# Last stores off GpSimd, two sums of one block on VectorE, one pair of loads on SyncE: attention and two MoE layers

## The chip, the cores and the metric

The kernel runs on one core of a Trainium2 chip. The time is that of one execution on the device in microseconds (us). TensorE (PE) multiplies matrices; VectorE (DVE), ScalarE (ACT) and GpSimd (POOL) compute on tiles; SyncE (SP), ACT and POOL issue the DMAs here.

## What is computed

Attention without a square score matrix, then two pairs of dense layers, on 4608 tokens (8 batches of 576), all in float32:

```
q_s = softmax(q over head_dim);  k_s = softmax(k over seq)
kv  = einsum('bhsd,bhse->bhde', k_s, v)
x   = einsum('bhsd,bhde->bhse', q_s, kv)  -> tokens x 512
h   = x @ moe_w_in   (512 -> 2048);  g = relu(h) ** 2;  y = g @ moe_w_out
h2  = y @ moe2_w_in  (512 -> 2048);  g2 = silu(h2);     out = g2 @ moe2_w_out
```

## The kernel before

Every float32 matrix is split into a high and a low part of a shorter type, and a product is three matmuls: high by high, low by high, high by low. The casts that make the high parts stand on ACT (names `ah`, `wh`, `wT`), the differences that make the low parts on DVE (`al`, `wl`, again `wT`).

**Stage one** is attention and the first dense layer, in NB = 9 blocks of tokens (i = 0 to 8), each NF = 16 steps on PE (`h<-x,wh` and its like). Beside the steps of a block run the attention of the next one and the work on the hidden layer of this one. A step's result goes through relu and square on ACT into a tile `gs` with seven slots: four quarters A11, A12, A21, A22 and three sums. The next layer multiplies in a scheme with seven products of quarters, and it wants these operand sums made beforehand: `g_first` (DVE) makes S1 = A21 + A22 and S3 = A11 − A21, `g_second` makes S2 = S1 − A11 and S4 = A12 − S2 on GpSimd, and `g_store` sends the tile, 896 KB, to DRAM (`g1d0` to `g1d7`) by a DMA that GpSimd issues. There are eight such pairs of sums a block, j = 0 to 7, at due steps 2j + 3, 2j + 4 and 2j + 5. Three tiles with two halves each are used in turn, so the ACT result of a later j waits until the store of an earlier one has landed. The last block's sums run on past the last step, into the next stage.

**The later stages** are the first layer's output (`x<-al,wT`, `d<-ah,wB`, steps of PE on stored tiles that come back by SP as `al<-g1d`), the second layer's input and its output. Here `wT`, `wB` and `wN` are weight sums; the raw ones (`wt`, `wB`) are made by GpSimd and DVE, and a low part is made by ACT and DVE just before its use. 

**The end.** The result of the last tokens comes back in two halves; each half is transposed by DVE into `st` and written by `store()` in 16 DMAs, over segments, quarters a and rows r. When `ends` is true (the last tokens), before gave four of them to GpSimd, and six each to ACT and SP; half 1 goes some 8 us ahead of half 0. Eight semaphores stand for the DMAs of SP and ACT together, so from the fifth store on a queue each waits for the landing of an earlier one.

**The start.** `r_load` brings the last 64 keys and values of every head of a batch (`kr`, `vr`); for batch 0 the two `kr` loads are issued by GpSimd and the two `vr` loads by ACT, ahead of the list `first_loads` ("q0 k1 v0 q1 w0 ...") on SP and ACT.

**The order.** Block 0 of stage one is ordered by a scheduler, which may move instructions on the engines for the sake of their inputs. From block 1 on, `pinned` keeps every instruction in the order in which the program issues it. All instructions are recorded by the helper `InOrder`, so they all carry its line, L73; closing ones carry L1276 (L1277 with the change), and tile names tell them apart.

Of the kernel before, what the change touches and what calls it, by code (L numbers as in the profile page):

```python
# [13 lines left out]
ALU = mybir.AluOpType  # L14
# [11 lines left out]
def kernel(  # L26
# [36 lines left out]
    class InOrder:  # L63
# [16 lines left out]
    ve, ac, gp, sp, pe = (  # L80
        InOrder(e) for e in (nc.vector, nc.scalar, nc.gpsimd, nc.sync, nc.tensor)
    )
# [7 lines left out]
    NB = NT // TB  # L90
# [31 lines left out]
    def room(dt=F32, name="u"):  # L122
        n = rooms.popleft()
        t = (upool if n < NU else rpool[0]).tile([P, TB], dt, tag=f"u{n}", name=name)
        lent[id(t)] = (t, n, rooms)
        return t
# [29 lines left out]
    S4, S2, S1, A21, A11, A22, A12 = range(7)  # L156
# [231 lines left out]
    def r_load(b, pr, dma=sp, dma2=sp):  # L388


        prs = range(KC)
        held[b] = [room(F32, "kr"), room(F32, "vr")]
        kr, vr = held[b][0], held[b][1][:, 0:KC * (D + 1)]
        n = len(prs)
        kr = kr.rearrange("p (c h d) -> p c h d", c=n, h=2)
        vr = vr.rearrange("p (c d) -> p c d", c=n)
        ms = ve if b == 0 else gp
        for j in range(2):
            ms.memset(kr[SR * j:SR * (j + 1), :, 1 - j, :], LOW)
        ms.memset(vr[:, :, D:D + 1], 1.0)  # L400
        for t, x in ((kr, k), (vr, v)):
            for j in range(2):
                o = slice(SR * j, SR * (j + 1))
                (dma if x is k else dma2).dma_start(
                    out=t[o, :, j, :] if x is k else t[o, :, 0:D],
                    in_=x[b, 2 * prs[0] + j:2 * prs[-1] + 2:2, SM:S, :].rearrange(
                        "c p d -> p c d"
                    ),
                )
        for c, x in enumerate(prs):  # L410
            krt[b, x], vrt[b, x] = kr[:, c], vr[:, c]

    def kv_load(b, pr, dma=sp):
        if pr == 0 and b > 0:
            kvf_room(b)
        hs = slice(2 * pr, 2 * pr + 2)
        kk = room(F32, "k")
        held[b, pr] = [kk]
        if b == 0:
            t = room(F32, "m")  # L420
            held[b, pr].append(t)
            m, mb = t[:, 0:2 * D], t[:, 2 * D:4 * D]
            v_rooms(b, pr)
        else:
            m, mb = input_room(b, pr)[:, 4 * D:6 * D], None
        kk = kk.rearrange("p (h r d) -> p h r d", h=2, r=R)
        dma.dma_start(out=kk, in_=k[b, hs, 0:SM, :].rearrange("h (p r) d -> p h r d", r=R))
        kt[b, pr] = kk
        if b > 0 and pr == 0:
            r_load(b, pr)  # L430
        mt[b, pr], mbt[b, pr] = m, mb
# [294 lines left out]
    def g_place(i, j):  # L726
        n = turns.index(j if i is None else (i, j))
        return g_tiles[n // 2 % 3][:, :, n % 2 * HB:(n % 2 + 1) * HB]
# [16 lines left out]

    def g_second(i, j):
        t = g_place(i, j)
        gp.tensor_tensor(t[:, S2], t[:, S1], t[:, A11], op=ALU.subtract)
        gp.tensor_tensor(t[:, S4], t[:, A12], t[:, S2], op=ALU.subtract)

    def g_store(i, j):
        o = slice(A21, 7) if i == 0 else slice(0, A21 + 1) if i is None else slice(0, 7)
# [25 lines left out]
    for i in range(NB):  # L778
        for j in range(NG):
            if i:  # L780
                at(i, 2 * j + 3, g_first, i, j)
                at(i, 2 * j + 4, g_second, i, j)
            at(i, 2 * j + (5 if i else 3), g_store, i, j)
            if (i, j) in AGAIN:
                again = AGAIN[i, j]
                at(i, 2 * j + 2, g_again, again)
                at(i, 2 * j + 5, g_first, None, again)
                at(i, 2 * j + 6, g_second, None, again)
                at(i, 2 * j + 7, g_store, None, again)
# [39 lines left out]
    def width(u):  # L829
        return sizes[u] * 2 * Q  # L830
# [87 lines left out]
    def hidden_after(ph, u, n, k, j):  # L918
# [39 lines left out]
        elif n == 5:  # L958
# [8 lines left out]
            def then():  # L967
                ve.tensor_tensor(at_("s1"), at_("c21"), at_("c22"), op=ALU.add)
                ve.tensor_tensor(at_("c21"), at_("c11"), at_("c21"), op=ALU.subtract)
                ve.tensor_tensor(at_("s2"), at_("s1"), at_("c11"), op=ALU.subtract)  # L970
                store((A22, "c22"), (S1, "s1"), (S3, "c21"), (A11, "c11"))
# [19 lines left out]
    def out_after(u, n, e, done):  # L991
# [4 lines left out]
        if n == 0:  # L996
            ac.copy(p0, p)
        elif n == 2:
            ac.copy(u2, p)
        elif n == 4:  # L1000
            ve.tensor_tensor(p0, p, p0, op=ALU.add)
            back(ps.pop(("a", e)))
            turn(u, 1, e, p0)
        elif n == 1:
            ac.copy(u3, p)
            d = ps["d", e][:, 0:w]

            def then():
                ve.tensor_tensor(u3, d, u3, op=ALU.add)
                turn(u, 0, 2 + e, u3)  # L1010
            later(then)
        elif n == 6:
            ve.tensor_tensor(u2, p, u2, op=ALU.add)
            back(ps.pop(("d", e)))
            turn(u, 1, 2 + e, u2)
            if e == 1:
                store(u, 1, done)
        elif n == 5:
            turn(u, 0, e, p)
            back(ps.pop(("x", e)))  # L1020
            if e == 1:
                store(u, 0, done)
# [10 lines left out]
    def store(u, half, ends):  # L1033
        w = width(u)
        t = st[half][:, 0:4].rearrange("p n c -> p (n c)")[:, 0:4 * w]
        n = 2 * Q
        for i in range(NB):
            m0, m1 = (max(0, min(w, i * HB + x - starts[u])) // n for x in (0, HB))
            if m0 == m1:
                continue  # L1040
            if i < B:
                lo = i * S + 2 * (starts[u] + m0 * n - i * HB)
                os = [(0, Q, out[lo:lo + 2 * n * (m1 - m0)].rearrange(
                    "(m j s r) (a f) -> a s r j m f", j=Q, s=2, r=2, f=P
                ))]
            else:
                b0 = 2 * ((starts[u] + m0 * n - i * HB) // n)
                rows = out[b0 * S:(b0 + 2 * (m1 - m0)) * S].rearrange(
                    "(m b t) (a f) -> b t m a f", b=2, t=S, f=P
                )  # L1050
                os = [
                    (b * Q // 2, Q // 2, rows[b, SM:S].rearrange("(j s r) m a f -> a s r j m f", s=2, r=2))
                    for b in range(2)
                ]
            for j, nj, o in os:
                for a in range(P // Q):
                    for r in range(2):
                        (gp if not ends or (a, r) in ((0, 0), (2, 1)) else ac if r else sp).dma_start(
                            out=o[a, half, r],
                            in_=t[a * Q + j:a * Q + j + nj].rearrange(  # L1060
                                "j (m r f) -> r j m f", r=2, f=P
                            )[r][:, m0:m1],
                        )
# [23 lines left out]

    warm = [spool.tile([P, 1], F32, name=f"warm{x}") for x in range(3)]
    kv_load(0, 0, ac)
    r_load(0, 0, gp, ac)  # L1090
    ve.memset(warm[0], 0.0)
    ve.memset(warm[2], 0.0)
    gp.partition_all_reduce(warm[1], warm[0], P, bass_isa.ReduceOp.max)
# [58 lines left out]
    for n in range(NB * NF + 6):  # L1152
        i, t = divmod(n, NF)
        ends = i >= NB - 1
# [126 lines left out]
```

## Time and profile before

| | |
|---|---|
| timed runs, median (lowest to highest), us | 1575.15 (1574.21 to 1580.14) |
| the profiled execution's own time, us | 1569.96 |
| its span from the first to the last instruction, us | 1568.1 |
| mean granted clock of PE | 0.994 |
| busy: PE, DVE, ACT, POOL | 97%, 72%, 58%, 40% |
| bytes moved | 419.58 MB, mean 268 GB/s |

The span is what the views of the trace show; the profiled execution's time is 1.86 us longer, and the median of the timed runs 5.19 longer than that. Views are cut to a stretch of time, since the shares of the whole span mix five stages. A row of waits names who waits, for whom, the total, the number and the longest. A row of a timeline gives start, length and, in brackets, the idle time before and what ended it. A group gives its count, busy time, the mean of one in ns, and idle time. PEld is the weight load of PE; a trailing q (SPq) is an engine's sequencer, which issues DMAs and closes the program.

### The profile page before, as it was taken

To read this page: it belongs to the slowest core of one execution; us is meant where nothing else is said; L and a number is where in the kernel's file an instruction comes from. 1 tells how busy PE (TensorE), PEld (TensorE's weight loads), DVE (VectorE), ACT (ScalarE), POOL (GpSimd) and SP (SyncE) were. 2 spreads that over 40 slices of the span, in tenths; PEclk is the share of its full clock that TensorE was granted. 3 is DMA by queue.
4 is the path that set the end of the run, shared out by engine and by line. 5 is a ranking of instruction groups with operands and counts; after the bars stand their busy time and mean duration, and the time that the engine had idled before them with its cause. 6 is when DMAs were issued, how large, how long until landed. Compare 5 with 4: busy or idle time off the path is not lost.

```text
span 1568.1 us, 25313 instructions
## 1 busy us (share of the span) xinstructions
PE 1527.3 (97%) x7679; PEld 1329.8 (85%) x7679; DVE 1125.8 (72%) x2263; ACT 907.0 (58%) x1927; POOL 625.2 (40%) x966
## 2 busy tenths in 40 slices
PE   5899999999999999999999999999999999999996
PEld 3678888888888899999988999999888899889995
DVE  7887888986627977767888776767757865564644
ACT  7876666666545755554575664555646744454431
POOL 1035556655659020211144544445485040605231
PEclk9999999999999999999999999999999999999998
DMA  8969999999977898989996776877889777868761
GB/s 216 287 204 286 310 326 312 328 328 298 333 242 240 292 309 271 331 274 328 304 318 224 245 285 245 297 272 261 310 290 315 235 237 200 247 182 240 207 228 47
DMA packets 270376, 419.58 MB, mean 268 GB/s; under 512 B 70272, under 2 KB 202496, under 8 KB 270240
## 3 DMA queue, kind: packets, MB, share of 16 engines
q1 hardware_dynamic: 216912, 246.39, 51.9%
q0 software_dynamic: 50976, 170.50, 30.0%
q10 hardware_dynamic: 2352, 1.08, 0.3%
q8 instruction: 60, 0.98, 0.3%
q14 instruction: 76, 0.62, 0.1%
HBM read 236.72 MB, written 181.14 MB: 266 GB/s over the span
## 4 chain that ended last, share of the span: by engine, by line
PE 91%; DVE 3%; DMA 2%; ACT 2%; issue 1%; POOL 1%; SPq 0%; POOLq 0%; ACTq 0%; DVEq 0%
PE x L73 37%; PE h L73 23%; PE d L73 19%; PE a L73 9%; PE kvps L73 2%; PE xps L73 2%; DVE wu L73 1%; ACT gs L73 0%; DMA al<-g2d 0%; DMA kr<-in_k_dram 0%; DMA wraw<-in_moe_w_in_dram 0%; DVE al L73 0%; DVE xr L73 0%; DMA g1d<-gs 0%; DMA g2d<-st 0%
## 5 line engine op out<-in xcount | busy, mean ns | idle before, releaser
L73 DVE TENSOR_TENSOR al<-al,ah 128x448 fp32r<-128x448 f32 (+1 forms) x630 | 374.6, 644 | 181.4 <-ACT ah L73 179.2
L73 ACT CAST ah<-al 128x448 fp32r<-128x448 f32 (+1 forms) x630 | 334.6, 577 | 143.6 <-PE x L73 54.1
L73 PE MATMUL h<-x,wh 128*128 128x512 f32 x1152 | 364.3, 396 | 1.3 <-ACT wh L73 0.7
L73 PE MATMUL x<-ah,wT 128*128 128x448 f32 (+1 forms) x960 | 287.3, 370 | 0.0
L73 PEld LDWEIGHTS h<-x,wh 128*128 128x128 f32 x1152 | 214.5, 189 | 47.2 <-ACT wh L73 1.2
L73 ACT COPY st<-x 128x448 f32<-128x448 f32 (+1 forms) x181 | 98.1, 543 | 248.5 <-PE x L73 237.2
L73 PE MATMUL h<-x,wl 128*128 128x512 f32 x576 | 225.9, 392 | 0.0
L73 PEld LDWEIGHTS x<-ah,wT 128*128 128x128 f32 x960 | 180.3, 188 | 19.8 <-ACT st L73 0.7
L73 POOL DMA_DIRECT2D out_dram<-st x184 | 96.6, 535 | 243.5 <-DVE st L73 237.0
L73 POOL DMA_DIRECT2D g2d<-st x262 | 140.8, 542 | 130.4 <-ACT st L73 64.1
L73 PE MATMUL x<-al,wT 128*128 128x448 f32 (+1 forms) x480 | 177.6, 370 | 0.0
L73 POOL TENSOR_TENSOR gs<-gs 128x256 f32<-128x256 f32 x144 | 124.2, 865 | 106.4 <-DVE gs L73 50.9
L73 ACT ACTIVATE gs<-h 128x512 f32<-128x512 f32 x144 | 86.0, 597 | 136.6 <-PE h L73 129.3
L73 PE MATMUL a<-ah,wB 128*128 128x448 f32 (+1 forms) x480 | 148.4, 370 | 0.0
L73 PE MATMUL x<-ah,wB 128*128 128x448 f32 (+1 forms) x480 | 144.7, 373 | 0.0
L73 PE MATMUL d<-ah,wB 128*128 128x448 f32 (+1 forms) x480 | 143.6, 370 | 0.0
L73 PE MATMUL d<-ah,wT 128*128 128x448 f32 (+1 forms) x480 | 143.5, 370 | 0.0
L73 PE MATMUL x<-ah,wN 128*128 128x448 f32 (+1 forms) x480 | 143.5, 370 | 0.0
L73 PEld LDWEIGHTS h<-x,wl 128*128 128x128 f32 x576 | 108.6, 189 | 23.6 <-issue 0.5
L73 DVE TENSOR_TENSOR st<-st 128x448 f32<-128x448 f32 (+1 forms) x161 | 100.0, 647 | 25.9 <-ACT st L73 21.0
L73 DVE TENSOR_TENSOR gs<-gs 128x256 f32<-128x256 f32 x144 | 74.9, 525 | 41.3 <-ACT gs L73 24.0
L73 PEld LDWEIGHTS x<-ah,wB 128*128 128x128 f32 x480 | 90.9, 189 | 9.7
(130 smaller groups left out, 2689.5 us busy)
## 6 DMA issues: line engine op xcount, KB each, us to landing
g1d<-gs POOLq DMA_DIRECT2D x64, 896.0 KB, 6.6
al<-g1d SPq DMA_DIRECT2D x224, 224.0 KB, 4.2
al<-g2d SPq DMA_DIRECT2D x224, 224.0 KB, 3.3
g2d<-st POOLq DMA_DIRECT2D x210, 224.0 KB, 3.7
al<-g1d SPq DMA_DIRECT2D x56, 256.0 KB, 4.2
al<-g2d SPq DMA_DIRECT2D x56, 256.0 KB, 3.1
g2d<-st POOLq DMA_DIRECT2D x52, 256.0 KB, 3.7
al<-x2d SPq DMA_DIRECT2D x56, 224.0 KB, 5.1
```

Of the source, the lines that this page charges most:

```text
L73: got = fn(*a, **kw)
```

## The change

The last tokens' stores go to SP and ACT alone, eight each a half. In the last block (i = 8) both sums of `g_second` stand on DVE. The two loads of the first batch's last keys go first on SP.

```diff
@@ g_second
     def g_second(i, j):
         t = g_place(i, j)
-        gp.tensor_tensor(t[:, S2], t[:, S1], t[:, A11], op=ALU.subtract)
-        gp.tensor_tensor(t[:, S4], t[:, A12], t[:, S2], op=ALU.subtract)
+        by = ve if i == NB - 1 else gp
+        by.tensor_tensor(t[:, S2], t[:, S1], t[:, A11], op=ALU.subtract)
+        by.tensor_tensor(t[:, S4], t[:, A12], t[:, S2], op=ALU.subtract)
@@ store
-                        (gp if not ends or (a, r) in ((0, 0), (2, 1)) else ac if r else sp).dma_start(
+                        (gp if not ends else ac if r else sp).dma_start(
@@ before block 0
     kv_load(0, 0, ac)
-    r_load(0, 0, gp, ac)
+    r_load(0, 0, sp, ac)
```

On POOL, at the end of the last block of stage one (480 to 515 us): `gs x2` are the two sums of one `g_second`, the `g1d` rows are the stores.

```order
 L73 DMA g1d1_128<-gs_186 896x1x256
-L73 TENSOR_TENSOR gs_187<-gs_187 128x256 x2
 L73 DMA g1d2_129<-gs_187 896x1x256
-L73 TENSOR_TENSOR gs_187<-gs_187 128x256 x2
 L73 DMA g1d3_130<-gs_187 896x1x256
-L73 TENSOR_TENSOR gs_188<-gs_188 128x256 x2
 L73 DMA g1d4_131<-gs_188 896x1x256
-L73 TENSOR_TENSOR gs_188<-gs_188 128x256 x2
 L73 DMA g1d5_132<-gs_188 896x1x256
-L73 TENSOR_TENSOR gs_186<-gs_186 128x256 x2
 L73 DMA g1d6_133<-gs_186 896x1x256
```

The sums leave, and the stores follow one another; each now waits for DVE. Ahead of this piece the store of the block before (`g1d7`), that of j = 0 and eight `wt` sums stand in a row, from between which two such pairs have gone.

The sums now stand on DVE, in the same stretch. The piece begins at the `wB` that waits for a `wt` of POOL; before:

```order
L73 TENSOR_TENSOR wB11_5205<-wB11_5205 128x256
L73 TENSOR_TENSOR wB11_5214<-wB11_5214 128x256
L73 TENSOR_TENSOR gs_187<-gs_187 128x256 x2
L73 TENSOR_TENSOR gs_188<-gs_188 128x256 x4
L73 TENSOR_TENSOR al_5352<-al_5352,ah_5440 128x448
L73 TENSOR_TENSOR al_5354<-al_5354,ah_5445 128x448
L73 TENSOR_TENSOR al_5373<-al_5373,ah_5467 128x448
L73 TENSOR_TENSOR al_5375<-al_5375,ah_5472 128x448
L73 TENSOR_TENSOR gs_186<-gs_186 128x256 x2
```

After:

```order
L73 TENSOR_TENSOR wB11_5205<-wB11_5205 128x256
L73 TENSOR_TENSOR wB11_5214<-wB11_5214 128x256
L73 TENSOR_TENSOR gs_187<-gs_187 128x256 x6
L73 TENSOR_TENSOR gs_188<-gs_188 128x256 x6
L73 TENSOR_TENSOR al_5352<-al_5352,ah_5440 128x448
L73 TENSOR_TENSOR al_5354<-al_5354,ah_5445 128x448
L73 TENSOR_TENSOR gs_188<-gs_188 128x256 x2
L73 TENSOR_TENSOR al_5373<-al_5373,ah_5467 128x448
L73 TENSOR_TENSOR al_5375<-al_5375,ah_5472 128x448
L73 TENSOR_TENSOR gs_186<-gs_186 128x256 x2
```

Eight sums become sixteen here. Further on, the last `gs` row ahead of `al_5416` (the `al` that the prediction calls the late one) is `x6` where it was `x2`, the rest stays; from the `wB` to that `al` there are 22 sums where there were 10.

On SP, the end of the program: the last load, then the stores of the two halves (`st_5530`, then `st_5529`).

```order
 L73 DMA al_16111<-g2d3_7_118 128x448
-L73 DMA out_0_dram<-st_5530 32x3x128 x3
-L73 DMA out_0_dram<-st_5530 32x4x128 x3
-L73 DMA out_0_dram<-st_5529 32x3x128 x3
-L73 DMA out_0_dram<-st_5529 32x4x128 x3
-L1276 UNCONDITIONAL_BRANCH
+L73 DMA out_0_dram<-st_5530 32x3x128 x4
+L73 DMA out_0_dram<-st_5530 32x4x128 x4
+L73 DMA out_0_dram<-st_5529 32x3x128 x4
+L73 DMA out_0_dram<-st_5529 32x4x128 x4
+L1277 UNCONDITIONAL_BRANCH
```

Each half has eight stores here in place of six, as on ACT; POOL's end loses its four a half. At the start of SP a row `DMA kr_199<-in_k_dram 64x4x64 x2` stands ahead of all loads, and the scheduler gives block 0 another order: on DVE, `x_335<-xps_332,x_334` of the first pair of heads now stands ahead of the second pair's `sm_345`.

## Rows read from the trace of the kernel before

**Rows 1.** The page's chain that ended last, by engine

```profile
PE 91%; DVE 3%; DMA 2%; ACT 2%; issue 1%; POOL 1%; SPq 0%; POOLq 0%; ACTq 0%; DVEq 0%
```

**Rows 2.** Waits of PE, 90 to 508 us (total, times, longest)

```profile
PE xps L73 <- ACT qh L73: 0.2, 1, 0.2
```

**Rows 3.** Waits of every engine, 490 to 530 us

```profile
ACT ah L73 <- DMA g1d<-gs: 6.8, 1, 6.8
...
PE x L73 <- DVE al L73: 3.5, 1, 3.5
```

**Rows 4.** Two stretches of PE: busy, granted clock, DMA share, GB/s

```profile
511.80:515.10 3.30, 3.30 (x11) 0.50 0.99 308
515.30:518.60 3.30, 3.30 (x18) 1.00 1.01 330
```

**Rows 5.** Timeline of DVE, 482 to 513 us: start, length, idle before

```profile
487.34 3.90 DVE L73 TENSOR_TENSOR wB<-wB 128x256 fp32r<-128x256 f32 x2 [11.22 <-POOL wt L73]
...
509.58 1.78 DVE L73 TENSOR_TENSOR al<-al,ah 128x448 fp32r<-128x448 f32 x1
```

**Rows 6.** Groups on DVE, 486 to 512 us: busy us, mean ns, idle

```profile
L73 DVE TENSOR_TENSOR gs<-gs 128x256 f32<-128x256 f32 x10 | 9.5, 969 | 0.2
L73 DVE TENSOR_TENSOR al<-al,ah 128x448 fp32r<-128x448 f32 x7 | 7.9, 1173 | 0.0
L73 DVE TENSOR_TENSOR wT<-wt,wT 128x256 fp32r<-128x256 f32 x5 | 4.0, 845 | 0.0
```

**Rows 7.** Groups on DVE, 515 to 535 us

```profile
L73 DVE TENSOR_TENSOR al<-al,ah 128x448 fp32r<-128x448 f32 x20 | 12.3, 615 | 0.0
L73 DVE TENSOR_TENSOR wT<-wt,wT 128x256 fp32r<-128x256 f32 x14 | 5.7, 415 | 0.0
```

**Rows 8.** Groups on POOL, 486 to 513 us

```profile
L73 POOL TENSOR_TENSOR gs<-gs 128x256 f32<-128x256 f32 x14 | 12.6, 897 | 0.6
...
L73 POOL TENSOR_TENSOR wt<-wB,wt 128x256 f32<-128x256 f32 x6 | 5.1, 909 | 0.0
```

**Rows 9.** Closing line L1276: ns min/median/max, first and last start

```profile
L1276 SPq EVENT_SEMAPHORE  x11: 17/28/28, 1560.3 to 1568.1; - x11
...
L1276 POOLq DRAIN  x3: 46/102/10698, 1556.7 to 1567.9; - x3
```

**Rows 10.** Waits of PE, 21 to 99 us

```profile
PE xps L73 <- ACT xr L73: 1.8, 1, 1.8
```

**Rows 11.** Timeline of POOL, 1545 to 1570 us

```profile
1546.80 2.19 POOL L73 DMA_DIRECT2D out_dram<-st  x4 [41.01 <-DVE st L73]
```

**Rows 12.** The output's stores, 1540 to 1570 us

```profile
L73 ACTq DMA_DIRECT2D out_dram<-st x12: 323/445/458, 1546.5 to 1557.8; - x12
...
DMA to landing us min/median/max: 1.6/2.9/3.4
```

**Rows 13.** Timeline of ACT, 1545 to 1557 us

```profile
1549.76 1.03 ACT L73 CAST ah<-al 128x448 fp32r<-128x448 f32 x2 [13.59 <-DMA out_dram<-st]
```

**Rows 14.** Timeline of DVE, 1549 to 1552.4 us

```profile
1550.36 1.16 DVE L73 TENSOR_TENSOR al<-al,ah 128x448 fp32r<-128x448 f32 x2 [3.85 <-ACT ah L73]
```

**Rows 15.** Timeline of the weight loads, 1551 to 1552.4 us

```profile
1551.72 0.19 PEld L73 LDWEIGHTS x<-al,wN 128*128 128x128 f32 x1
```

**Rows 16.** Timeline of DVE, 440 to 460 us

```profile
445.64 0.89 DVE L73 TENSOR_TENSOR gs<-gs 128x256 f32<-128x256 f32 x2 [2.88 <-ACT gs L73]
```

**Rows 17.** Timeline of POOL, 480 to 515 us

```profile
482.94 0.82 POOL L73 DMA_DIRECT2D g1d<-gs  x1
...
506.26 0.90 POOL L73 DMA_DIRECT2D g1d<-gs  x1 [0.30 <-DVE wT L73]
```

**Rows 18.** The page's DMA issues: KB each, us to landing

```profile
g1d<-gs POOLq DMA_DIRECT2D x64, 896.0 KB, 6.6
```

**Rows 19.** Tile kr, 0 to 40 us

```profile
L73 POOL DMA_DIRECT2D kr<-in_k_dram x2: 626/694/761, 1.3 to 2.0; - x2
```

**Rows 20.** The chain that ended last, 0 to 36 us: start, length

```profile
2.04 6.95 DMA kr<-in_k_dram
```

## Prediction

> **What bounds the kernel now.** The chain of waits by engine comes first: 91% of the span is PE's own work [rows 1], so a gain on another engine counts only where PE waits for it or where PE is done. The list of PE's waits then tells where those places are. From 90 to 508 us there is nothing above 0.2 us [rows 2]: whatever the start loses or wins goes through to the end one for one. Between 490 and 530 us there is one real hole, where PE waits 3.5 us for an `al` of VectorE, and beside it ScalarE waits 6.8 us for a store of the hidden tiles [rows 3]. The hole has an echo: in the 3.3 us after it the granted clock is 0.50, 1.2 GHz, and 11 matmuls fit in where the next 3.3 us, at 2.4 GHz, hold 18 [rows 4].
>
> Why VectorE is late there is read from its timeline and its groups. It sat 11.22 us behind a `wt` of POOL until 487.34, and the late `al` ends at 509.58 + 1.78 = 511.36; so 24.0 us of work stand between [rows 5]. That work is slow: an `al` takes 1173 ns and a `wT` 845 [rows 6], against 615 and 415 some 20 us later [rows 7], when POOL computes nothing. In the slow stretch POOL ran 14 sums on the hidden tiles, 12.6 us, and its `wt` sums [rows 8]. The two engines slow each other.
>
> The end is the third place. SyncE begins its closing waits, for the stores' landings, at 1560.3, but a DRAIN on POOL that begins at 1556.7 lasts 10,698 ns, to 1567.4 [rows 9]; the span ends 0.7 later, at 1568.1. So the last 6 us hold no work at all. The start is the fourth: PE has single waits of up to 1.8 us before 99 us [rows 10].
>
> The profiled execution took 1569.96 us, its span 1568.1; the median of the timed runs is 1575.15, 5.19 above it. I work in the profiled execution's time and take the difference off the median.
>
> **Part 1, the last stores.** POOL's eight go; its last DMA then ends 41.01 us ahead of 1546.80 [rows 11], and a DRAIN of some 11 us from there is over near 1517, while PE still works. What sets the end instead are the stores of the last half on SyncE and ScalarE, eight each instead of six. ScalarE issues six in the time from 1546.5 to 1549.76 [rows 12, 13], 0.54 each (445 ns for the issue itself, the rest waits for an earlier store). Its last one was issued at 1557.8; two more make it 1558.9, and with the median landing of 2.9 us [rows 12] the data are there at 1561.8. SyncE's closing waits, eleven of 28 ns [rows 9], and the 0.7 of closing make about 1562.8: −5.3. With the longest landing, 3.4, it is −4.8; with an issue every 445 ns, −5.5.
>
> The Trainium skill speaks against this part: "VectorE: DVE Perf Modes", section "The DRAIN you can't avoid", says that the DRAINs of a program's preamble and postamble are about 12 ns on every engine, whatever the kernel. By that nothing would be won here, for the stores' move would take away no such wait, and the sum would be that of the first rival. The trace does not agree, with its 10,698 ns on POOL.
>
> The first half's stores are the cover that may be lost. ScalarE's two casts for the last steps stand behind its six stores, until 1549.76 [rows 13]; two more stores make it 1550.84. The `al` that follows begins at 1550.36 [rows 14], and PE loads from it at 1551.72 [rows 15]. The first of the two is done after about 0.58, at 1550.94, so 0.78 is spare and 1.08 is asked: +0.3. Its bounds are 0.1 (two issues at 445 ns, 0.89) and 1.1 (no slack).
>
> **Part 2, two operand sums of the last block.** Of VectorE's work between its release and the late `al` the new order makes 22 sums on `gs` instead of 10; the 7 `al`, 4 `wT` and 2 `wB` stay. At undisturbed prices, 0.89 for a pair of sums [rows 16], 615 and 415 ns [rows 7] (a `wB`, of the same shape, as a `wT`), that is 9.8 + 4.3 + 1.7 + 0.8 = 16.6 us, against the 24.0 it took with fewer. The release comes earlier: POOL's store at 482.94 [rows 17] is followed at once by the next, 0.82 + 0.90, and then by the `wt` that VectorE waits for, 0.9 [rows 8]: 485.6 instead of 487.34. POOL has seven more `wt` to do, at 0.85 each (5.1 for six), until about 491.5, and after that it only issues stores. In those 6 us VectorE goes at 445/969 of its pace [rows 6, 16], 2.8 us of the 16.6, and the rest alone: the `al` is there at 491.5 + 13.8 = 505.3. PE asks for it at 511.4 − 3.5 = 507.9. If VectorE is blocked altogether until 491.5, it is 508.1. So the wait goes, or leaves 0.2.
>
> What is late next is the store that ScalarE waited for: issued at 506.26 [rows 17], with a median of 6.6 to landing [rows 18] there at 512.9. Its pair of sums now stands on VectorE behind the two `wB`, six other pairs and two `al`; with it that is 0.8 + 6.2 + 1.2 = 8.2 us of the 16.6, so 496.9 (499.7 blocked), then 0.9 for the issue and 6.6 to landing: 504.4 (507.2), and a cast and an `al`, about 0.6 each, later 505.6 (508.4). PE wants this one at least 1.5 us after the first, since today it comes that much later and no wait is listed: 509.4. It fits, with 1.0 to spare in the blocked case.
>
> With the wait goes the slow clock behind it: 3.3 us at 1.2 GHz do the work of 1.65. Part 2 gives 3.5 + 1.7 = −5.2; bounds −5.2 and, by the rival below, +9.9.
>
> The Trainium skill has a mechanism for the mutual slowing: "SBUF — State Buffer", section "SBUF: two separate sides", calls the port pair that VectorE and GpSimd share an exclusive lock, where one instruction blocks the other for its whole length. The trace bears this out (1173 against 615 ns). By the lock alone the blocked case, 508.1, would be the forecast, 0.2 us worse.
>
> **Part 3, the first keys.** The two loads, issued by POOL at 1.3 and 2.0, each some 0.69 [rows 19], are now the first two on SyncE, from about 0.75. The second then goes out near 1.45 instead of 2.04 and, with the same 6.95 to landing [rows 20], gives up to 0.6. It pushes every other load of SyncE back by 1.4, the first q and k among them. Block 0 is ordered by a scheduler, and VectorE now takes a result of the first pair ahead of the second pair's sums, so a part of what is won is handed on as a wait. No row shows the new order: at best the longest wait before 99 us goes, −1.8 [rows 10]; at worst one like it comes on top of the 1.4, +3.2. I take +0.5, near the middle, on the side of the 1.4 that is certain.
>
> **Sum:** −5.3 + 0.3 − 5.2 + 0.5 = −9.7: the profiled execution at 1560.3, the median at 1565.4.
>
> **Rivals.**
> *The DRAIN follows the stores.* It is POOL's, but it may wait for every DMA of the program: it ended 6.7 us after the last landing, 1557.8 + 2.9 = 1560.7. Then the end is 1561.8 + 6.7 + 0.7 = 1569.2, and part 1 costs 1.1. Sum −3.3: 1571.9. For it, that the trace ties the DRAIN to nothing; against it, that only POOL has such a long one. The skill's constant DRAIN of part 1 would come out on this side too.
> *VectorE stays late.* POOL's eight `wt` now come as one block, and the `al` may still miss its time; at the same 3.5 and 1.7 the sum is −4.5: 1570.7. For it, that the blocked case is already 0.2 over; against it, the 615 ns as soon as POOL is quiet.
> *The start is worse* by the whole 3.2: −7.0, 1568.2. For it, the 1.4 on SyncE; against it, that the chain of the start runs through these very keys [rows 20].
> *VectorE becomes the bound, slower than before.* If the sums' 969 ns are not POOL's doing but the price of this stretch, 12 more cost 11.6, less the 1.7 of earlier release: +9.9 instead of −5.2. The sum is −5.3 + 0.3 + 9.9 + 0.5 = +5.4: 1580.6. It decides the sign once the `al` comes more than 4.5 us later than 511.4. Against it, the pair at 0.89 in the same stage [rows 16].
>
> **Chances.** Forecast 0.62, DRAIN follows 0.10, VectorE late 0.13, start worse 0.12, VectorE the bound 0.03. The likeliest case has its own range of 1562 to 1568, from −1.8 for the start and −5.5 for the end up to +3.2. For 8 in 10 the range takes in the DRAIN and the late VectorE: 1561 to 1572. The bound of 0.5% is 7.9 us, which a measurement here can just tell from no change: 1567.3 is faster, 1583.0 slower. The forecast case clears it in nine of ten, 0.56; two of the other cases with a better start or end add 0.02. Slower in the strict sense needs the last rival at a worse price: 0.02. Same: 0.40.
>
> **What the profile would show.** Part 1: the long DRAIN on POOL begins near 1506 in the old time, and the closing waits on SyncE are the last thing; if a DRAIN still ends 6 us behind them, the first rival. Part 2: no wait of PE for `al` between 500 and 520 us, clock 1.00 throughout, `gs` and `al` on VectorE near 445 and 615 ns after POOL's last `wt`; a PE wait with `al` still above 1 us while POOL only issues stores speaks for the last rival. Part 3: block 1's first matmul comes 0.5 later, and PE's waits before 99 us change place. The prediction is wrong if PE shows a new wait elsewhere, or if the start moves by more than 3.

## The result and the profile after

| | before | after |
|---|---|---|
| timed runs, median, us (six each) | 1578.99 | 1562.86 |
| lowest to highest, us | 1574.21 to 1580.14 | 1559.99 to 1568.81 |
| ratio of the times | | 0.9909, 95% interval 0.9885 to 0.9933 |
| profiled execution, us (span) | 1569.96 (1568.1) | 1560.76 (1559.0) |
| mean granted clock | 0.994 | 0.999 |

The change makes the kernel 0.9% faster; 1565.4 was forecast, in a range from 1561 to 1572. From profile to profile the span falls by 9.1 us, where 9.7 was the sum. That the two lie so close is in part luck: a loss that was not forecast stands against larger gains elsewhere. The timed ratio, taken over the same rounds, says 14 us (11 to 18 by its interval); the difference is taken up below. The medians lie 16 us apart, since the six runs of before have a median of 1578.99 where the first three had 1575.15.

The same matmul, matched in both traces, gives the account by place:

| place | matmul before | earlier after | gained here |
|---|---|---|---|
| block 1 under way | 105.8 | 1.03 | 1.0 |
| end of stage one | 497.5 | 1.03 | 0 |
| next stage | 527.7 | 5.68 | 4.7 |
| later stages | 1221.6 | 5.56 | −0.1 |
| 120 us on | 1342.0 | 3.21 | −2.4 |
| last steps | 1553.1 | 3.17 | 0 |
| end of the span | 1568.1 | 9.1 | 6.0 |

**The stage's end.** PE's waits from 500 to 560 us, after (total, times, longest), hold nothing of the 3.5 us any more [rows 3]:

```profile
PE d L73 <- DVE al L73: 0.2, 1, 0.2
```

VectorE's timeline there, after (start, length, idle before), answers to [rows 5]:

```profile
485.61 5.41 DVE L73 TENSOR_TENSOR wB<-wB 128x256 fp32r<-128x256 f32 x2 [7.99 <-POOL wt L73]
490.94 4.86 DVE L73 TENSOR_TENSOR gs<-gs 128x256 f32<-128x256 f32 x12
...
504.24 0.62 DVE L73 TENSOR_TENSOR al<-al,ah 128x448 fp32r<-128x448 f32 x1
```

And its groups, 482 to 512 us (count, busy us, mean ns), to [rows 6]:

```profile
L73 DVE TENSOR_TENSOR gs<-gs 128x256 f32<-128x256 f32 x22 | 8.7, 422 | 0.4
L73 DVE TENSOR_TENSOR al<-al,ah 128x448 fp32r<-128x448 f32 x11 | 6.6, 620 | 2.3 <-ACT ah L73 2.3
L73 DVE TENSOR_TENSOR wB<-wB 128x256 fp32r<-128x256 f32 x2 | 5.4, 2745 | 8.0 <-POOL wt L73 8.0
```

The sums went from 969 ns to 422, the `al` from 1173 to 620. The means of before mix two kinds: of the seven `al` that stood in this stretch some took 0.61 us, the price of a quiet stretch, and others up to 1.79. The 2745 ns of the two `wB` after are such a mean too. The tile's rows (ns min/median/max), `al` before and then `wB` after:

```profile
L73 DVE TENSOR_TENSOR al<-al,ah x7: 611/1151/1785, 497.2 to 509.6; 128x448 fp32r<-128x448 f32 x7
```

```profile
L73 DVE TENSOR_TENSOR wB<-wB x2: 414/2745/5076, 485.6 to 490.6; 128x256 fp32r<-128x256 f32 x2
```

Only the first `wB` is slow, 5076 ns; the second takes 414. The slow one stands where POOL still makes its `wt` sums; POOL's timeline after shows the end of these and the first store behind them:

```profile
485.95 4.44 POOL L73 TENSOR_TENSOR wt<-wB,wt 128x256 f32<-128x256 f32 x6
490.11 1.14 POOL L73 DMA_DIRECT2D g1d<-gs  x1
```

VectorE's first `wB` lasts from 485.61 to 490.68 and POOL's row of six sums ends at 485.95 + 4.44 = 490.39, so one instruction of VectorE stood through the whole row. From then on no instruction of VectorE in the stretch is stretched. The granted clock stays 1.00 through the place where it was 0.50 [rows 4]; the windows of PE after (length, busy, clock, DMA share, GB/s):

```profile
506.90:510.00 3.10, 2.92 (x14) 1.00 1.01 346
511.00:515.00 4.00, 4.00 (x21) 1.00 0.94 255
```

The 0.18 us missing in the first of them is a small new lag. The chain of waits after, 495 to 515 us, names it:

```profile
498.19 10.06 DMA g1d<-gs
...
508.40 0.58 ACT ah L73
...
509.00 0.64 DVE al L73
...
509.68 5.35 PE d L73 x25
```

A store of the hidden tiles takes 10.06 us to land, and the cast and `al` that need it are done at 509.64, just too late for PE. The matched matmuls put its price at about 0.5: 6.29 earlier at 508.73 of after's time, 5.74 at 510.39.

**The end.** The closing line, after (ns min/median/max, first and last start), against [rows 9]:

```profile
L1277 SPq EVENT_SEMAPHORE  x11: 17/28/28, 1555.6 to 1558.9; - x11
...
L1277 POOLq DRAIN  x3: 46/93/9845, 1502.0 to 1558.7; - x3
```

POOL's DRAIN is still 9.8 us long, but it begins at 1502.0, beside PE's work. Now SyncE's waits end last. The stores after, and ScalarE's part of them:

```profile
L73 ACTq DMA_DIRECT2D out_dram<-st x16: 322/440/457, 1543.4 to 1555.4; - x16
...
DMA to landing us min/median/max: 1.6/2.1/2.4
```

```profile
1547.20 1.04 ACT L73 CAST ah<-al 128x448 fp32r<-128x448 f32 x2 [14.21 <-DMA out_dram<-st]
1551.86 3.84 ACTq L73 DMA_DIRECT2D out_dram<-st  x8
```

Eight stores take 3.84 us, 0.48 each, and land after 2.1 where it was 2.9 [rows 12].

**The start.** PE's waits before 95 us, after; `kvps<-ACT k` and `kvf` have taken the places of [rows 10]:

```profile
PE xps L73 <- ACT kvf L73: 2.8, 3, 1.3
PE kvps L73 <- ACT k L73: 2.3, 1, 2.3
```

The granted clock differs as well. From 40 to 60 us before had 3.4 us at 0.50, after none; PE's windows, before and then after:

```profile
40.00:60.00 20.00, 16.61 (x117) 0.91 1.15 317
```

```profile
40.00:60.00 20.00, 17.17 (x127) 1.00 1.13 305
```

### The profile page after: what moved, and what is told of

Read it like the earlier page. It is cut to its first block, busy times and chain, and to the rows that moved or that the text cites. A ratio compares the mean times of both kernels' runs of the same rounds, so it can differ in the third digit from the quotient of the medians.

```text
span 1559.0 us, 25288 instructions
## 1 busy us (share of the span) xinstructions
PE 1528.6 (98%) x7679; PEld 1327.1 (85%) x7679; DVE 1123.3 (72%) x2279; ACT 906.1 (58%) x1927; POOL 607.7 (39%) x940
## 4 chain that ended last, share of the span: by engine, by line
PE 94%; DVE 2%; DMA 2%; ACT 1%; issue 0%; SPq 0%; POOL 0%; ACTq 0%; DVEq 0%
PE x L73 37%; PE h L73 24%; PE d L73 19%; PE a L73 10%; PE kvps L73 2%; PE xps L73 2%; DMA g1d<-gs 1%; DVE st L73 0%; ACT q L73 0%; DVE al L73 0%; DMA wraw<-in_moe_w_in_dram 0%; DMA q<-in_q_dram 0%; PE qps L73 0%; DVE wT L73 0%; DVE wu L73 0%
## 5 line engine op out<-in xcount | busy, mean ns | idle before, releaser
L73 POOL DMA_DIRECT2D out_dram<-st x176 | 92.2, 532 | 198.6 <-DVE st L73 192.4
L73 POOL TENSOR_TENSOR gs<-gs 128x256 f32<-128x256 f32 x128 | 111.3, 871 | 104.6 <-DVE gs L73 49.9
L73 PEld LDWEIGHTS d<-ah,wB 128*128 128x128 f32 x480 | 90.1, 188 | 10.0 <-DVE st L73 0.2
```

Of the source, the lines that this page charges most:

```text
L73: got = fn(*a, **kw)
```

## Experiments

All ratios are to the kernel before in the same rounds, with a 95% interval. The theory: the three parts act in three places and add; POOL's arithmetic holds VectorE, and POOL's own last DMA sets its DRAIN. Each edit is given against the kernel named.

**Part 1 alone** (against before):

```diff
-                        (gp if not ends or (a, r) in ((0, 0), (2, 1)) else ac if r else sp).dma_start(
+                        (gp if not ends else ac if r else sp).dma_start(
```

> Only the last stores change: none on GpSimd, sums and keys as before. If the long closing DRAIN belongs to GpSimd's own last DMA (theory), it ends beside PE's work near 1517, the time from PE's last matmul to the end falls from 13.8 us by 5.5 to 6, PE's waits before 1550 us stay those of before (3.5 us near 508), and the ratio of the times is near 0.996. If the DRAIN waits for every DMA of the program (rival), a DRAIN still ends some 6 us after SyncE's closing waits and the time is that of before or 1 us above.

Measured: 0.9960 (0.9944 to 0.9977). The DRAIN began at 1512.7, 9,743 ns long. From the last steps to the end the span lost 6.3 us: the last steps came 5.98 later than in the first profile of before, the end 0.3 earlier. The theory holds and the first rival falls. PE waited 4.1 us near 508, as nothing there was changed, and the slow clock behind it lasted longer than before, which the windows of PE show:

```profile
512.00:515.10 3.10, 2.67 (x7) 0.50 0.97 303
515.30:518.40 3.10, 3.10 (x10) 0.50 1.02 358
518.80:521.90 3.10, 3.10 (x17) 1.00 1.01 367
```

**Part 2 alone** (against before):

```diff
-        gp.tensor_tensor(t[:, S2], t[:, S1], t[:, A11], op=ALU.subtract)
-        gp.tensor_tensor(t[:, S4], t[:, A12], t[:, S2], op=ALU.subtract)
+        by = ve if i == NB - 1 else gp
+        by.tensor_tensor(t[:, S2], t[:, S1], t[:, A11], op=ALU.subtract)
+        by.tensor_tensor(t[:, S4], t[:, A12], t[:, S2], op=ALU.subtract)
```

> Only the two sums of the last block go to VectorE. Theory (GpSimd and VectorE slow each other): PE's wait near 508 us and the slow clock behind it go, 4 to 5.3 us, ratio near 0.997; the sums take near 450 ns once GpSimd only issues stores. Rival (VectorE becomes the bound): PE waits over 3.5 us for al near 508, time up to 5 us longer.

Measured: 0.9931 (0.9910 to 0.9952), a span of 1562.6 us. Its PE has no wait near 508 and no slow clock; the matched matmuls gain 4.6 us there (0.49 earlier at 497.5, 5.08 at 527.7), and the sums take 421 ns. The mechanism holds. The timed gain, 11 us (8 to 14), is larger than the profile's 5.5, and the expected ratio of 0.997 lies outside the interval.

**Part 3 alone** (against before):

```diff
-    r_load(0, 0, gp, ac)
+    r_load(0, 0, sp, ac)
```

> Only the first keys go first on SyncE. Theory: the whole effect lies before block 1, its first matmul is 0.5 to 1.5 us earlier than 99.05, ratio near 0.9995, not to be told from no change. Rival (the delayed q and k loads cost more): first matmul of block 1 later than 99.05. A third: if the clock's first full stretch comes at another time here, up to 2 us more or less.

Measured: 0.9993 (0.9975 to 1.0012): no change that can be told. Block 1 began 0.3 earlier, where 0.5 to 1.5 was expected. The first matmuls on q (`qps`) start at 13.01, 2.0 us earlier than before; the next two groups of them come 0.9 and 1.8 later, and by 100 us the 0.3 is left. The profile holds no low clock from 40 to 60 us. The third case of the expectation, that the clock moves, is taken up with part 3 below.

**The whole change, a second time**:

> The changed kernel once more, with a second profile. If the three places are all there is, its time against before in the same rounds is 9 to 11 us shorter (ratio 0.993 to 0.994). If the first timing, 0.9909, was no chance, 14 us shorter, and a further place must show in which before's timed executions lose 4 to 5 us more than its profiled one. The matmuls' pace of 206.7 ns between 1218 and 1336 us is not part of the change if this profile has it elsewhere or not at all; if it has it at the same place, it is.

Measured: 0.9915 (0.9889 to 0.9942), span 1558.2. So the first ratio came again within 0.001, though this interval still takes in 0.993 to 0.994, what the three places alone would make. The pace of 206.7 ns, the mean distance of two matmuls of 448 columns where it is 202.7 elsewhere, is not the change's: this profile lacks it. The view of two windows shows it by the number of matmuls; after:

```profile
600.00:660.00 60.00, 60.00 (x297) 1.00 0.92 312
1240.00:1300.00 60.00, 60.00 (x292) 1.00 0.76 223
```

and the second profile of the same kernel:

```profile
1240.00:1300.00 60.00, 60.00 (x298) 1.00 0.78 234
```

PE is busy throughout at clock 1.00 in both, and yet does 292 or 298 matmuls in 60 us.

**Parts 1 and 2 without part 3**:

```diff
-    r_load(0, 0, sp, ac)
+    r_load(0, 0, gp, ac)
```

> The changed kernel without its third part (first keys stay on GpSimd). If the parts add as they did alone (0.996 and 0.9931), the ratio is 0.989, 17 us, below the whole change's 0.9915, and the third part costs up to 3 us in company. If the third part is worth nothing either way, the ratio is 0.990 to 0.992 and the profile of PE from block 1 on is that of the whole change within 1 us.

Measured: 0.9911 (0.9889 to 0.9933), six runs from 1558.22 to 1561.95, span 1556.4, the shortest of all. The second expectation holds: the third part is worth nothing that the timing shows. The single ratios of parts 1 and 2, 0.9960 and 0.9931, would make 0.989; the interval holds that too.

**The first half's stores on SyncE alone** (against after):

```diff
-                        (gp if not ends else ac if r else sp).dma_start(
+                        (gp if not ends else sp if half else ac if r else sp).dma_start(
```

> The changed kernel, with all 16 stores of the first half on SyncE, none on ScalarE. If ScalarE's two more stores there cost PE time (prediction, 0.3 us), PE's end comes up to 0.3 earlier; if they cost nothing, PE's end stays. SyncE then issues until some 7.5 us after the first half's transposes and may be late for the second half's: up to 1 us later at the end. Time within 1 us of the whole change, ratio 0.991 to 0.992.

Measured: 0.9935 (0.9912 to 0.9957), some 3 us more than the whole change where within 1 us was expected, inside both intervals. PE gained nothing at the end, so ScalarE's two more stores had cost nothing. From PE's last steps to the end it took 1.0 us longer than after, with SyncE issuing 24 stores without a pause, as expected. Another 5 us of this profile are the slow pace in a longer stretch, 292 matmuls from 600 to 660 us.

**One store kept on POOL** (against after; one of the last half's sixteen):

```diff
-                        (gp if not ends else ac if r else sp).dma_start(
+                        (gp if not ends or (not half and m1 - m0 == 3 and a == 0 and r == 0) else ac if r else sp).dma_start(
```

> The changed kernel with one single store of the last half kept on GpSimd. If the DRAIN runs some 10 us from GpSimd's own last DMA, whatever their number (theory), it ends about 10.5 us after that store, the span from PE's end to the end is 11 to 13 us instead of 7.9, and the time 4 us longer than the whole change. If the DRAIN's length goes by the number of late DMAs (rival, eight made 10.7), one makes 1.4 us and nothing changes at the end.

Measured: 0.9958 (0.9941 to 0.9975). The closing line of this kernel:

```profile
L1277 SPq EVENT_SEMAPHORE  x11: 17/28/28, 1553.4 to 1560.8; - x11
...
L1277 POOLq DRAIN  x3: 46/93/9885, 1550.2 to 1560.6; - x3
```

One DMA makes a DRAIN of 9,885 ns, as eight made 10,698. It runs from 1550.2, beside that store, to 1560.1, and the span ends at 1560.9; SyncE was through its waits at 1556.0. The rival (length by number) falls. The profile is 1.9 us longer than after while PE's last steps come 1.9 earlier: 3.8 us, as expected. The timed ratio has it some 7 us above the whole change.

**One of the two sums on VectorE** (against after):

```diff
-        by.tensor_tensor(t[:, S4], t[:, A12], t[:, S2], op=ALU.subtract)
+        gp.tensor_tensor(t[:, S4], t[:, A12], t[:, S2], op=ALU.subtract)
```

> The changed kernel, but only the first of the two sums of the last block goes to VectorE, the second stays on GpSimd. Theory (GpSimd's arithmetic blocks VectorE): eight GpSimd sums still stand between its stores, 7 us, VectorE's sums and al in the stretch take well over 450 and 620 ns, and PE waits 1 to 4 us for al near 508, with a stretch of slow clock behind it. Rival (the place of the work alone matters, VectorE's own pace is the bound): VectorE has fewer sums than in the whole change and PE does not wait.

Measured: 0.9925 (0.9897 to 0.9953), not to be told from the whole change. A miss: PE waited 0.3 us, not 1 to 4, and the clock stayed up.

```profile
PE x L73 <- DVE al L73: 0.3, 1, 0.3
```

The stretching is there, but smaller than I had reckoned. VectorE's groups, 484 to 512 us:

```profile
L73 DVE TENSOR_TENSOR gs<-gs 128x256 f32<-128x256 f32 x16 | 8.7, 576 | 0.2
L73 DVE TENSOR_TENSOR al<-al,ah 128x448 fp32r<-128x448 f32 x11 | 7.1, 666 | 0.7 <-ACT ah L73 0.7
L73 DVE TENSOR_TENSOR wB<-wB 128x256 fp32r<-128x256 f32 x2 | 6.1, 3091 | 9.7 <-POOL wt L73 9.7
```

With half of POOL's sums a sum on VectorE takes 576 ns on average, between 422 and 969, and an `al` 666. Here too the mean hides two kinds: half of the 16 sums took 416 ns or less, and the longest 1273.

```profile
L73 DVE TENSOR_TENSOR gs<-gs x16: 410/416/1273, 491.3 to 504.6; 128x256 f32<-128x256 f32 x16
```

So the direction of the theory is borne out, and its size not; that PE does not wait is also what the rival said. This run alone doesn't tell them apart. Half the move would have been nearly enough.

**The kernel before, a second and a third profile**:

> The kernel before, word for word, for a second profile. Open is why the two sums alone won 10.9 us in the timed runs (7.6 to 14.2) where the profile of before holds 5.2 to 5.7 for them. If the profiled execution of before was a mild one, this one shows the slow clock behind the wait near 508 us for 6.8 us instead of 3.4 (1.7 us more), or matmuls at 206.7 ns a step in a stretch of the later stages where the first has 202.7, and its span is 1570 to 1576. If it was typical, the span is within 1 us of 1568.1 and the surplus stays unexplained.

> The kernel before once more, a third profile, for the same question: the length of the slow clock behind the wait near 508 us (3.4 or 6.8 us) and how long PE steps at 206.7 ns.

Measured: spans of 1570.9 and 1569.7 us. In both the slow clock lasts 3.4 us, as in the first, so that isn't it. Both have the slow pace from about 1227 to 1342 us, which the first profile of before lacks and the first of after has. Before's second profile:

```profile
1240.00:1300.00 60.00, 60.00 (x292) 1.00 0.79 240
```

**Every sum of the last block made twice on VectorE** (against parts 1 and 2):

```diff
-        by.tensor_tensor(t[:, S2], t[:, S1], t[:, A11], op=ALU.subtract)
-        by.tensor_tensor(t[:, S4], t[:, A12], t[:, S2], op=ALU.subtract)
+        for _ in range(2 if i == NB - 1 else 1):
+            by.tensor_tensor(t[:, S2], t[:, S1], t[:, A11], op=ALU.subtract)
+            by.tensor_tensor(t[:, S4], t[:, A12], t[:, S2], op=ALU.subtract)
```

> Stores and sums as changed, keys as before; and every sum of the last block is made twice on VectorE, 12 more between its release and the al for which PE waited. VectorE was 2.0 us ahead there in the changed kernel (al at 504.9, wanted at 506.9). Theory (VectorE's pace alone at 405 to 450 ns a sum): the al comes 4.9 to 5.3 later, PE waits 2.9 to 3.3 us near 508 and the slow clock comes back behind it, 1.7 to 3.4 us; time 4 to 7 us above stores and sums alone, ratio 0.994 to 0.996. Rival (VectorE has more slack than it seems, the al's are held by other things): no PE wait over 1 us, time the same.

Measured: 0.9963 (0.9940 to 0.9987). PE's waits from 500 to 560 us:

```profile
PE x L73 <- DVE al L73: 3.4, 1, 3.4
```

3.4 us, a little over the 2.9 to 3.3 expected, and 3.4 us of clock 0.50 behind them (514.35 to 517.76). VectorE's lead of some 2 us was real, and this is where "VectorE becomes the bound" begins: between 2 and 5 us of added work, not at zero. The ratio lies just above the expected 0.994 to 0.996. Of the 16.0 us by which this profile is longer than that of parts 1 and 2, this place holds 5.1; 9.1 are the slow pace in the later stages and 1.8 the start.

**The sums of the last two blocks on VectorE** (against parts 1 and 2):

```diff
-        by = ve if i == NB - 1 else gp
+        by = ve if i is not None and i >= NB - 2 else gp
```

> Stores as changed, keys as before, and the sums of the last two blocks on VectorE. VectorE is busy 4.5 of 20 us between 440 and 460, so 16 more sums should cost PE nothing, and GpSimd is free earlier for the wt that VectorE waits for. Theory: the small waits for al near 510 (0.2 to 0.5 us) go, time 0 to 1 us below stores and sums alone, ratio 0.990 to 0.991. Rival (VectorE becomes the bound where it works beside GpSimd's wt): a PE wait for al or x between 440 and 510, time 1 to 5 us longer.

Measured: 0.9921 (0.9906 to 0.9937), runs from 1558.89 to 1561.29, span 1556.9. PE's waits from 500 to 560 us are none, and the matched matmuls gain 5.35 there (0.44 earlier at 495.9, 5.79 at 541.1) instead of 4.65. The small lag of after is gone, as the theory said; 0.7 us are too few for the timing. So no version beats parts 1 and 2 by what can be measured.

## Why the prediction was right, point by point

**Part 1, −5.3 and +0.3.** Right in mechanism: the DRAIN belongs to POOL's own last DMA and hides beside PE. In size 6.0 instead of 5.0 net. No run has POOL end on anything but a DMA, so whether other work at its end would start such a DRAIN is not shown. The stores were a little faster than priced (0.48 for an issue instead of 0.54, 2.1 to landing instead of 2.9), and the 0.3 for the first half did not come: the casts began at 1547.20, and the last steps have no wait in the list. The slack was there because eight stores took 3.84 us where six had taken 3.23: 0.61 more, with 0.78 spare, where 1.08 was priced. The price of 0.54 rested on six stores that ended in a wait for an earlier landing. That this wait shrinks with faster landings is argued, and why they are faster without GpSimd's queue was not tried.

**Part 2, −5.2.** Measured −4.65, in the other profiles with both sums moved −4.1 to −5.35. Up to 508.73 it was 6.29 − 1.03 = 5.26, as forecast, and the new lag took the rest. Its steps can be checked one by one, with 1.0 taken off each forecast time, since after started earlier. The release, then 484.6, came at 485.61, 1.0 late; POOL's last `wt`, then 490.5, ended at 490.39, in time. That VectorE would go on at 46% beside the `wt` sums was wrong: 2.8 us of its work were to be done by then, and it did the two `wB`, 0.8, which is the blocked case. The 46% came from the means of before, which mix free instructions with held ones. Against that, VectorE's instructions follow one another closer than their lengths say, twelve sums in 4.86 us, 405 ns each. The two errors nearly cancel, which is luck: the `al` was done at 504.24 + 0.62 = 504.86, in after's time, and 505.3 − 1.0 was forecast. The trace thus sides with the exclusive lock in "SBUF — State Buffer" of the Trainium skill (section "SBUF: two separate sides") at this place: 5.08 us for a sum of 0.41, and 422 ns a sum as soon as POOL only issues stores. It goes further than the one instruction that by this page blocks the other: the sum of VectorE stood through a row of six on POOL.

What failed is "what is late next". I had the store landing after the median of 6.6 us. Five stores now go out within 8 us, where one went out every 3 us before, and their landings after are 6.5, 6.7, 8.1, 9.7 and 10.06 us, in this order. The run with every sum made twice speaks for the bunch as the cause: its stores go out 2.5 to 3.6 us apart there and land after 5.7 to 7.1. The `al` behind the last of the five was done at 509.64, where 508.4 − 1.0 = 507.4 was my blocked case, and PE lost some 0.5 there.

**Part 3, +0.5.** Wrong in sign in the profile (−1.0), inside its bounds; the timing tells neither. The six profiles with the keys on SyncE have block 1 between 1.85 earlier and 0.28 later than the first of before (mean 0.8 earlier), the other seven, before's two among them, between 0.49 earlier and 1.60 later (mean 0.2 later). The start scatters by more than this part is worth. The scatter goes with the clock, for which the prediction had no term here. All eight profiles with the keys on POOL have 3.4 or 6.8 us at a granted clock of 0.50 between 44 and 54 us; of the six with the keys on SyncE four have none in the start, and two have 3.4 there and 3.4 more from 25 us on. Block 1 came 1.0 earlier on average without low clock, 0.3 with 3.4 us of it, and 0.3 later with 6.8. So the profiles lean to a gain of about 1 us; with so few it is not shown, and what makes the clock fall there stays open.

**The pace, not forecast, +2.4.** Between 1221 and 1342 us after lost 2.4 us with no wait, at full granted clock. It is not the change's: it comes in two of before's three profiles and one of the whole change's two. The sum came out at 9.1 because this loss stood against part 1 (1.0 better than forecast) and part 3 (1.5 better); part 2 was 0.5 worse.

**From 9.1 to 14 us.** Mean spans of three profiles each are 1569.6 (before: 1568.1, 1570.9, 1569.7) and 1557.9 (after 1559.0, its second 1558.2, parts 1 and 2 1556.4): 11.7 us, inside the interval of the ratio. So a part of the gap was that before's first profile was a mild one. Before's own timed median moved from 1571.6 to 1579.0 between the rounds, so the difference of two such means is rough. A further part may lie in the wait itself: two of the kernels that have it, part 1 and part 3 alone, showed 6.8 us of slow clock behind it instead of 3.4, 1.7 us more. And the slow pace filled some 34 to 459 us of the six profiles with the wait (mean about 215) and 0 to 257 of the eight without (mean about 83); at 2% that is 4.3 against 1.7 us. With so few profiles that is an argument and not shown. What starts the slow pace stays open.

**The rivals.** "DRAIN follows the stores" fell with part 1 alone and with the single store. "VectorE stays late" fell with PE's waits. "VectorE the bound" is real, but beyond 2 us of added work.

## What to carry to other kernels

Read the closing lines of a profile: in these kernels the DRAIN on GpSimd that outlasted the last landing went by its own last DMA, and it cost nothing once that lay well ahead of the others'. Where two engines do elementwise work in one stretch, price each instruction by a stretch where the other is quiet before saying which of them is the bound, and look at the shortest and the longest of a group, not at its mean; here moving work onto the late engine made it early. And stores that are moved into a bunch are priced by the bunch, not by the median landing.

## What the runs showed of the hardware

- GpSimd's DRAIN at the end was 9.7 to 10.7 us long in every profile, whether it began some 57 us ahead of the end or 11, and whether its last DMA was one of eight or alone. That is far from the 12 ns that the Trainium skill gives for such a DRAIN ("VectorE: DVE Perf Modes", section "The DRAIN you can't avoid").
- PE has two paces for the same 448-column matmuls at full granted clock and without a wait: 202.7 and 206.7 ns a step. A slow stretch begins at some point, and where several profiles have it, it ends at the same matmul of the program in all of them (about 518 to 783 us in the profile of part 3 alone; 865 to 904 and 1218 to 1338 us after). One is worth up to 5 us, and they make a part of the scatter of the times.
- The low clock (0.50) behind the wait near 508 us lasted 3.4 us behind waits of 3.4 to 4.0 us in four profiles, and 6.8 us behind the two waits of 4.1; behind waits under 0.6 in that place there was none.
- One sum on VectorE (`wB`) took 5076 ns beside a row of six sums on POOL and was done 0.3 us after the row; the next one, beside a DMA issue of POOL, took 414. Where POOL's row had gaps, in before, the same first `wB` took 3022.
